# Modulation and queries of a decode head: 224 matmuls of 8 columns replaced by wide weight streams on column groups, then turned by selection matmuls

## Chip, cores, metric

One core of one Trainium2 chip. The metric is the device time of one launch in microseconds (us), as a median of several runs; lower is better. All timed runs quoted here were in the same, undisturbed state ("fast"); runs with a single look are named as such. The profile is of one execution; its span is about 1.8 us shorter than the timed figure. In the profile, TensorE's matmuls are PE, its weight loads PEld, VectorE is DVE, ScalarE is ACT, GpSimd is POOL, and SPq is the sync engine's queue that issues nearly all transfers. L374 is a line of the kernel's source.

## The reference, cut to what matters

A transformer block at decode: batch 8, one new token each, width 512, 32 query heads on 8 key/value heads of 128, a cache of 8192 positions, all in bfloat16.

```python
mod = (silu(c) @ w_mod).reshape(8, 6, 1, 512)      # w_mod: 512 x 3072, 3.15 MB
sa, ca, ga, sb, cb, gb = mod[:, 0], ..., mod[:, 5]
h = layernorm(x) * (1 + ca) + sa
q = h @ wq                                         # wq: 512 x 4096, 4.19 MB
x = x + ga * (attention(q, k_cache, v_cache) @ wo) # caches: 134 MB each
h = layernorm(x) * (1 + cb) + sb
x = x + gb * ((relu(h @ w1 + b1) ** 2) @ w2 + b2)
```

The "head" is everything up to `q`. After it comes a loop over the batch: the keys are transposed on TensorE and multiplied by the queries, then softmax, then the values.

## The kernel before

Keys and values stream through a ring of four slots of 4 MiB. The head borrows slots 2 and 3 for `w_mod` and `wq`, so the loads of keys 2 and 3 wait until the head has read them. The order of the sync queue is: `w_mod`, `wq`, keys 0, keys 1, biases, two loads of `wo`, keys 2, keys 3, then values 0 and so on.

```python
# each output column block of 128 is a stationary operand; 8 columns (the batch) stream past it
for j in range(24):
    for k in range(KT):                                   # KT = 4
        t = op("tensor", lambda e, j=j, k=k: e.matmul(
            modT_ps[:, j, :], wm_cols(k, j), csT[:, k, :],
            start=(k == 0), stop=(k == KT - 1)), [k_csT, d_wm])
released[2] = t
k_modT = op("vector", lambda e: e.tensor_copy(modT[:], modT_ps), [t])
...  # [cut] haT = layernorm(x).T * (1 + ca) + sa, three small DVE operations
for h in range(HQ):
    for k in range(KT):
        t = op("tensor", lambda e, h=h, k=k: e.matmul(
            QT_ps[:, h, :], wq_v[:, k, h * DH:(h + 1) * DH], haT[:, k, :],
            start=(k == 0), stop=(k == KT - 1)), [k_haT, d_wq])
released[3] = t
...  # [cut] eight copies QT_ps -> QTm on DVE
stg_free = [None, None, None, k_QTm]    # one of the four PSUM buffers of the key transposes waits for the last copy into QTm
load(0); load(1)
...  # [cut] loads of biases and wo
load(2); load(3)                        # wait for released[2], released[3]
```

## Time and profile before

| | before |
|---|---|
| time, median | 670.73 us (670.6 to 670.85, 3 runs) |
| bytes read from HBM | 283.66 MB |
| rate from 40 to 640 us | 431 GB/s |
| modulation matmuls | 2.93 us |
| query matmuls | 3.56 us |
| last copy into QTm ends | 26.44 us |
| first key transposes start | 31.80 us |

First the page's line of the granted TensorE clock, the busy share of the 16 transfer engines and the rate, each in 40 equal slices of the span (16.7 us each; 9 is 90% or more):

```profile
PEclk9996995699869997699967997589966999689986
DMA  9999999999999999999999999999999999999996
GB/s 375 430 404 427 431 427 437 434 425 433 433 433 427 432 433 435 431 429 429 435 435 425 434 433 432 427 431 433 439 433 423 428 439 435 421 433 435 437 408 259
...
HBM read 283.66 MB, written 0.01 MB: 424 GB/s over the span
```

The same by stage, from the view of windows: after the stretch and its length come the busy time and number of instructions of PE, PEld, DVE, ACT and POOL, the granted clock, the DMA share and GB/s.

```profile
4.00:20.00 16.00, 4.13 (x108) 3.79 (x108) 3.31 (x12) 1.18 (x2) 11.08 (x34) 1.00 1.02 435
20.00:40.00 20.00, 11.75 (x240) 10.79 (x240) 5.99 (x19) 4.10 (x4) 2.79 (x14) 1.00 0.98 418
40.00:640.00 600.00, 460.39 (x6720) 314.02 (x6720) 282.96 (x514) 226.93 (x270) 0.00 (x0) 0.86 1.01 431
```

Transfers fill every stretch, the head too. TensorE is busy 460 of the 600 us of the loop, so it has room; the transfers have none. Dividing says what to expect of the head: 283.66 MB at 431 GB/s take 658 us, and the span is 668.8.

The head in the view of time (start, length, engine, line, operation; in brackets how long the engine was idle before, and what it waited for):

```profile
4.07 19.10 SPq L408 DMA_DIRECT2D wo_sb<-in_A_wo_dram  x1
...
11.47 2.93 PE L374 MATMUL PS<-csT,ring 128*128 128x8 bf16 x96 [0.19 <-DMA ring<-in_w_mod_dram]
...
15.27 0.19 DVE L382 TENSOR_TENSOR haT<-tmpT,modT 128x32 bf16<-128x32 f32 x1
...
21.97 3.56 PE L386 MATMUL PS<-haT,ring 128*128 128x8 bf16 x128 [7.57 <-DMA ring<-in_A_wq_dram]
23.21 22.55 SPq L335 DMA_DIRECT2D ring<-in_A_k_cache_dram  x2
...
25.56 0.88 DVE L392 CAST QTm<-PS 128x32 bf16<-128x32 f32 x8 [10.10 <-PE PS L386]
...
31.80 5.41 PE L429 MATMUL PS<-IDENT,ring 128*128 128x128 bf16 x64 [6.28 <-DMA ring<-in_A_k_cache_dram]
```

Read the brackets: both matmul stages begin when their weights land, and the key transposes begin when the keys land, 5 us after QTm is ready. And read the two SPq lines: the queue issues the second `wo` load at 4.07 us and does not get past it until 23.17 us, then stays in the loads of keys 2 and 3 until 45.76 us. The first of these alone takes 21.68 us (the same view, cut off at 32 us, shows it by itself), so keys 3 are issued at about 44.9 us, although slot 3 is free at 25.53 us.

The chain of waits, in order of time, up to the start of the first long work on TensorE that it holds: nothing of the head is in it.

```profile
1.26 0.42 SPq L266
1.68 0.05 issue
1.73 59.99 DMA ring<-in_A_k_cache_dram x2
```

### The profile page before, as it was taken

The page shows a single profiled execution, that of the slowest core. Times are in us where ns is not written, and L with a number is a line of the kernel's source. Part 1 is how long each engine was busy: PE and PEld are TensorE (multiplying, and loading weights), DVE is VectorE, ACT ScalarE, POOL GpSimd, SP SyncE. Part 2 cuts the span into 40 slices and gives each one's busy share as a digit, 9 for nine tenths or more (in the row PEclk, how much of TensorE's full clock was granted, in tenths as well). Part 3 has the DMA queues.
Part 4 walks back from the last instruction along what each step waited for, and adds up shares of the span by engine and source line. Part 5 has one row for each costly group of instructions (what it writes and reads, how often), then busy time and mean ns, then how long its engine had stood idle before and what let it go on. Part 6 is the DMA issues. An engine that isn't in the chain of part 4 may idle for free.

```text
span 668.8 us, 16189 instructions
## 1 busy us (share of the span) xinstructions
PE 495.9 (74%) x7492; PEld 341.4 (51%) x7492; DVE 298.8 (45%) x567; ACT 235.1 (35%) x280; POOL 16.9 (3%) x66
## 2 busy tenths in 40 slices
PE   2394964799639983699647996399846996489976
PEld 2383731676318751477316762287414772167634
DVE  2162741466316661267414672166613673156722
ACT  2061630365106640166204660056402662046600
POOL 7200000000000000000000000000000000000000
PEclk9996995699869997699967997589966999689986
DMA  9999999999999999999999999999999999999996
GB/s 375 430 404 427 431 427 437 434 425 433 433 433 427 432 433 435 431 429 429 435 435 425 434 433 432 427 431 433 439 433 423 428 439 435 421 433 435 437 408 259
DMA packets 12969, 283.95 MB, mean 425 GB/s; under 512 B 1266, under 2 KB 2323, under 8 KB 4372
## 3 DMA queue, kind: packets, MB, share of 16 engines
q1 hardware_dynamic: 12900, 283.65, 99.1%
q8 instruction: 13, 0.21, 0.1%
q14 instruction: 8, 0.07, 0.0%
q10 hardware_dynamic: 48, 0.02, 0.0%
HBM read 283.66 MB, written 0.01 MB: 424 GB/s over the span
## 4 chain that ended last, share of the span: by engine, by line
PE 50%; DMA 39%; DVE 5%; ACT 2%; SPq 2%; issue 1%
DMA ring<-in_A_k_cache_dram 37%; PE PS L429 36%; PE PS L444 9%; DVE Pm L533 3%; PE PS L561 2%; DMA ring<-in_B_w_dram 2%; SPq L602 2%; ACT KTb L434 1%; ACT P_sb L511 1%; DVE m L449 1%; PE PS L520 1%; PE PS L420 1%; PE PS L540 0%; DVE rhs_r L537 0%; DVE Dm L502 0%
## 5 line engine op out<-in xcount | busy, mean ns | idle before, releaser
L434 ACT ACTIVATE KTb<-PS 128x1024 bf16<-128x1024 bf16 x192 | 196.7, 1024 | 375.9 <-PE PS L429 375.9
L429 PE MATMUL PS<-IDENT,ring 128*128 128x128 bf16 x4096 | 267.3, 227 | 51.6 <-DMA ring<-in_A_k_cache_dram 51.6
L429 PEld LDWEIGHTS PS<-IDENT,ring 128*128 128x128 bf16 x4096 | 246.7, 102 | 100.3 <-DMA ring<-in_A_k_cache_dram 53.6
L436 DVE COPY KTb<-PS 128x1024 bf16<-128x1024 bf16 x320 | 210.2, 688 | 151.6 <-PE PS L429 149.2
L561 PE MATMUL PS<-ring,Pm 128*32 128x512 bf16 x992 | 83.3, 495 | 63.2 <-DMA ring<-in_A_v_cache_dram 62.3
L570 DVE CAST O_sb<-PS 128x512 bf16<-128x512 f32 x31 | 21.4, 692 | 144.5 <-PE PS L561 144.5
L444 PE MATMUL PS<-KTb,Qb 128*32 128x512 bf16 x1024 | 79.1, 386 | 4.5 <-ACT KTb L434 4.5
L561 PEld LDWEIGHTS PS<-ring,Pm 128*32 128x32 bf16 x992 | 29.5, 116 | 101.9 <-DMA ring<-in_A_v_cache_dram 63.6
L420 PE MATMUL PS<-IDENT 128*128 128x512 bf16 x120 | 31.3, 380 | 0.0
L574 PEld LDWEIGHTS PS<-SEL,O_sb 128*128 128x128 bf16 x124 | 5.3, 99 | 45.3 <-DVE O_sb L570 45.3
L511 ACT ACTIVATE P_sb<-PS,negm 128x512 bf16<-128x512 f32 x32 | 21.6, 686 | 18.9 <-DVE negm L507 18.9
L574 PE MATMUL PS<-SEL,O_sb 128*128 128x8 bf16 x124 | 8.0, 170 | 24.8 <-DVE O_sb L570 24.8
L444 PEld LDWEIGHTS PS<-KTb,Qb 128*32 128x32 bf16 x1024 | 15.4, 94 | 21.1 <-ACT KTb L434 8.5
L533 DVE COPY Pm<-PS 64x512 bf16<-64x512 bf16 x48 | 19.5, 419 | 13.4 <-PE PS L520 12.4
L449 DVE TENSOR_REDUCE m<-PS 128x1 f32<-128x512 f32 x32 | 22.1, 689 | 6.6 <-PE PS L444 6.6
L520 PE MATMUL PS<-IDENT,P_sb 128*64 128x128 bf16 x512 | 20.4, 222 | 2.0 <-ACT P_sb L511 1.2
L520 PEld LDWEIGHTS PS<-IDENT,P_sb 128*64 128x64 bf16 x512 | 15.2, 109 | 9.8 <-ACT P_sb L511 9.8
L420 PEld LDWEIGHTS PS<-IDENT 128*128 128x128 bf16 x120 | 9.9, 103 | 10.8 <-issue 3.4
L577 DVE TENSOR_TENSOR oTn<-PS,rinv 128x8 bf16<-128x8 f32 x31 | 6.0, 194 | 10.9 <-PE PS L574 10.9
L530 ACT ACTIVATE Pm<-PS 64x512 bf16<-64x512 bf16 x16 | 9.5, 593 | 1.1
L386 PE MATMUL PS<-haT,ring 128*128 128x8 bf16 x128 | 3.6, 168 | 7.6 <-DMA ring<-in_A_wq_dram 7.6
L668 ACT ACTIVATE std<-PS,epst 128x8 f32<-128x8 f32 x1 | 0.3, 268 | 25.1 <-PE PS L667 25.1
(112 smaller groups left out, 98.8 us busy)
## 6 DMA issues: line engine op xcount, KB each, us to landing
ring<-in_A_k_cache_dram SPq DMA_DIRECT2D x32, 4096.0 KB, 34.9
ring<-in_A_v_cache_dram SPq DMA_DIRECT2D x31, 4096.0 KB, 28.2
ring<-in_A_wq_dram SPq DMA_DIRECT2D x1, 4096.0 KB, 20.6
ring<-in_w_mod_dram SPq DMA_DIRECT2D x1, 3072.0 KB, 10.6
wo_sb<-in_A_wo_dram SPq DMA_DIRECT2D x1, 3072.0 KB, 45.4
ring<-in_A_v_cache_dram SPq DMA_DIRECT2D x1, 2048.0 KB, 23.6
ring<-in_B_w_dram SPq DMA_DIRECT2D x3, 512.0 KB, 17.5
ring<-in_B_w_dram SPq DMA_DIRECT2D x1, 1344.0 KB, 21.1
```

Of the source, the lines that this page charges most:

```text
L420: op("tensor", lambda e: e.matmul(bank(at).rearrange("p (a r) -> p a r", a=4), IDENT[:, :], rhs))
L429: t = op("tensor", lambda e, j=j, i=i: e.matmul(STG[j][:, i, :], src[:, 32 * k + 8 * j + i, :], IDENT[:, :], is_transpose=True), [loaded[n ...
L434: stg_free[j] = op("scalar", lambda e, j=j, dst=dst: e.activation(dst, STG[j], ACT.Copy), [t], "scaP")
L436: stg_free[j] = op("vector", lambda e, j=j, dst=dst: e.tensor_copy(dst, STG[j]), [t], "vecP")
L444: t = op("tensor", lambda e, hf=hf, q=q, rhs=rhs: e.matmul(PS[32 * q:32 * (q + 1), k, :], Qb[:, 2 * p + hf, :], rhs, start=(p == 0 and hf ...
L449: return op("vector", lambda e: e.tensor_reduce(m4[:, k:k + 1], bank(k), AX.X, ALU.max), [t])
L511: exps.append(op("scalar", lambda e, k=k: e.activation(P_sb[:, k, :], bank(k), ACT.Exp, bias=negm[:, 0:1], scale=inv_sqrt, accum_out=rs4[: ...
L520: t = op("tensor", lambda e, k=k, i=i, hf=hf, src=src: e.matmul(STG[k][64 * hf:64 * (hf + 1), i, :], src, IDENT[:, :], is_transpose=True, ...
L533: done.append(op("vector", lambda e, dst=dst, frm=frm: e.tensor_copy(dst, frm), [t, k_pm], "vecP"))
L561: t = op("tensor", lambda e, p=p, m=m, cg=cg, vt=vt, Obank=Obank: e.matmul(Obank[32 * cg:32 * (cg + 1), :], lhs[:, p, 32 * m:32 * m + 32], ...
L570: t = op("vector", lambda e, osb=osb, Obank=Obank: e.tensor_copy(osb, Obank), [t], "vecP")
L602: d_w2 = [dma("sync", s_w2[i], lambda e, a=a, z=z, j=j: e.dma_start(W2v[:, a:z, :].rearrange("p (k j) n -> p k (j n)", j=j), B_w2[128 * a: ...
```

## The change

Its intent: few wide matmuls in place of many narrow ones. The batch of 8, padded to 32, becomes the stationary operand and the weights stream past it, 512 columns at a time, on four column groups of the array at once. The result has batches on partitions, in four groups of 32 rows, and must be turned: a copy from PSUM to SBUF, then matmuls against a small selection matrix with ones at the 8 used rows of each group. Modulation does this in fp32, queries in bf16.

```diff
-        for j in range(24):
+        def row_groups(out_ps, lhsT, w, chunks, deps):
             for k in range(KT):
-                t = op("tensor", lambda e, j=j, k=k: e.matmul(
-                    modT_ps[:, j, :], wm_cols(k, j), csT[:, k, :],
-                    start=(k == 0), stop=(k == KT - 1)), [k_csT, d_wm])
+                for g, n in enumerate(chunks):
+                    t = op("tensor", lambda e, k=k, g=g, n=n: e.matmul(
+                        out_ps[32 * g:32 * (g + 1), :], lhsT[:, k, :], w[:, k, 512 * n:512 * (n + 1)],
+                        start=(k == 0), stop=(k == KT - 1), tile_position=(0, 32 * g)), deps)
+            return t
+
+        t = row_groups(bank(0), csT, wmod_v, (0, 1), [k_csT, d_wm])
+        k_mr0 = op("vector", lambda e: e.tensor_copy(mod_r[0:64, 0, :], bank(0)[0:64, :]), [t])
+        t = row_groups(bank(1), csT, wmod_v, (2, 3, 4, 5), [])
         released[2] = t
+        k_mr1 = op("scalar", lambda e: e.activation(mod_r[:, 1, :], bank(1), ACT.Copy), [t])
+        for i in range(KT):
+            t = op("tensor", lambda e, i=i: e.matmul(
+                mod_ab[:, :, i, :], mod_r[0:64, 0, :].rearrange("r (p i) -> r i p", i=KT)[:, i, :],
+                EYE[0:64, 0:2, :]), [k_mr0, k_xT])
 ...  [cut: copies, haT as before; a second selection for the other four chunks, weights mod_r[:, 1, 128*i:128*(i+1)]]
-        for h in range(HQ):
-            for k in range(KT):
-                t = op("tensor", ...)           # 128 matmuls
-        released[3] = t
+        t0 = row_groups(bank(2), haT, wq_v, (0, 1, 2, 3), [k_haT, d_wq])
+        released[3] = t = row_groups(bank(3), haT, wq_v, (4, 5, 6, 7), [])
+        k_q = [op("vector", lambda e: e.tensor_copy(q_r[:, 0, :], bank(2)), [t0]),
+               op("scalar", lambda e: e.activation(q_r[:, 1, :], bank(3), ACT.Copy), [t])]
+        for u in range(2):
+            for i in range(4):
+                t = op("tensor", lambda e, u=u, i=i: e.matmul(
+                    QT_ps[:, u, :, i, :], q_r[:, u, DH * i:DH * (i + 1)], EYEB[:, :, :]), [k_q[u]])
 ...  [cut: the eight copies into QTm; memsets and two selects on POOL for EYE, EYEB and the padding]
```

The loop, the loads, their order and their sizes are untouched.

## The prediction

> **What bounds the kernel now.** The page says that the kernel reads 283.66 MB at a mean of 424 GB/s. The windows view gives 431 GB/s from 40 to 640 us (DMA share 1.01), 435 from 4 to 20 us and 418 from 20 to 40 us: the head already streams at about the steady rate. 283.66 MB at 431 GB/s is 658 us of a span of 668.8; the rest is some 2 us of start and 5 us after the last weights. The Trainium skill, "DMA: Bandwidth & Descriptors", section "Where 436 GB/s comes from", puts the fabric at 435.2 GB/s; the trace agrees. So the bound is bytes, not the head's arithmetic.
>
> **The head in the timeline.** The 96 modulation matmuls take 2.93 us (11.47 to 14.40), as soon as w_mod has landed. TensorE idles 7.57 us for wq, and the 128 query matmuls take 3.56 us (21.97 to 25.53); eight copies into QTm end at 26.44. TensorE then idles 6.28 us until the first keys land at 31.8. The chain of waits holds none of this: its first piece of work is 59.99 us of key loads, from 1.73 us.
>
> **Do earlier releases start transfers earlier?** Slots 2 and 3 are released by the modulation and the query matmuls. But the sync queue is held in the second Wo issue from 4.07 to 23.17, and in the next two loads until 45.76, by transfers ahead of it; its list of waits names neither stage. Slot 2 is free 9 us before the queue gets to it, slot 3 (25.53) probably before its issue too. No DMA gap stands in the head that an earlier release could close.
>
> **What the change does.** It removes 224 matmuls of 8 columns (6.5 us of TensorE). It adds 56 matmuls of 32x512 on four column groups, 16 selection matmuls, two copies a stage (about 0.69 us each, as the 128x512 evictions take; one on DVE, one on ACT), and memsets and selects on GpSimd (estimated 1.5 us from its 0.1 to 0.45 us instructions). The same 32x512 form takes 1.91 us per 32 in the value stage, so I estimate modulation at 1.5 to 2 us, fp32 selection at 0.65 us (as the four fp32 transposes), haT at about 15 us instead of 15.5. Queries: 21.95 + 1.9 + 0.7 + 0.3 + 0.9, QTm complete at about 25.8. Slot 2 is released about 1 us earlier, slot 3 about 1.5 us. Loop, loads, their order and sizes are unchanged.
>
> **On the critical path:** none. Even a stage 4 us slower would end before the keys land. Net: 0 us, perhaps 0.1 us from fewer instructions or other phases of the transfers.
>
> **Predicted:** 670.6 us, 669.4 to 671.8 for 8 in 10. Faster by over 2%: 0.01; within 2%: 0.98; slower: 0.01.
>
> **What would show it right:** the query matmuls shrink from 3.56 to about 1.9 us, QTm is ready around 25.8 us, TensorE's idle time before the first key transposes grows from 6.3 to about 7 us; they still start at about 31.8 us; the Wo issue still lasts to about 23.2; key loads still take about 35 us from issue to landing; 40 to 640 us stays at 431 GB/s.
>
> **What would make it wrong:** a fall in GB/s in the loop (another phase between releases and loads); the sync queue waiting for slot 3 today; the dense 512-column matmuls lowering the granted clock later (0.70 in 60 to 70 us already) so far that slots are released late; copies and selections over 6 us longer than estimated.

## The result, and the profile after

The changed kernel takes 670.8 us (670.7 to 671.03, 4 runs), beside 670.79 us for the kernel before in the same rounds: ratio 1.0001, 95% interval 0.9984 to 1.0018. A ratio here is the mean of one kernel's fast runs over the mean of the other's of the same rounds, so not quite the ratio of the medians. The prediction (670.6 us, no change) holds. Its account of the head's inside does not.

The page after, same lines:

```profile
PEclk9696996799859995599968997699977999779985
DMA  9999999999999999999999999999999999999996
GB/s 375 434 405 437 415 435 433 432 427 433 433 437 428 427 437 431 433 429 431 435 435 428 427 433 437 427 429 433 435 437 428 423 435 439 429 427 433 435 410 250
...
HBM read 283.66 MB, written 0.01 MB: 424 GB/s over the span
```

The windows after:

```profile
4.00:20.00 16.00, 7.71 (x52) 4.92 (x52) 4.15 (x14) 1.77 (x3) 11.61 (x32) 0.96 1.03 441
20.00:40.00 20.00, 13.01 (x153) 9.50 (x154) 6.85 (x20) 4.69 (x5) 3.15 (x16) 0.69 0.97 415
40.00:640.00 600.00, 458.98 (x6716) 313.52 (x6716) 282.50 (x514) 226.75 (x270) 0.00 (x0) 0.87 1.00 431
```

The rate of the loop is 431 GB/s in both. But look at the first number after the length: TensorE is busy longer in the head than before (7.71 against 4.13 us, 13.01 against 11.75), with far fewer instructions. (About half of the second difference is only that the key transposes begin 0.7 us earlier.) The view of time shows why:

```profile
4.10 18.88 SPq L430 DMA_DIRECT2D wo_sb<-in_A_wo_dram  x1
...
11.34 3.60 PE L377 MATMUL PS<-ring,KTb 128*32 128x512 bf16 x24
...
14.87 2.04 PE L391 MATMUL PS<-EYE,KTb 64*128 64x16 f32 x8
...
16.83 1.08 PE L400 MATMUL PS<-EYE,KTb 128*128 128x32 f32 x8
...
17.64 0.19 DVE L398 TENSOR_TENSOR KTb<-tmpT,modT 128x32 bf16<-128x32 f32 x1
...
21.65 3.61 PE L377 MATMUL PS<-ring,KTb 128*32 128x512 bf16 x32 [3.74 <-DMA ring<-in_A_wq_dram]
...
23.03 23.01 SPq L344 DMA_DIRECT2D ring<-in_A_k_cache_dram  x2
...
26.26 0.88 DVE L414 CAST QTm<-PS 128x32 bf16<-128x32 f32 x8 [1.97 <-PE PS L410]
...
31.08 5.97 PE L451 MATMUL PS<-IDENT,ring 128*128 128x128 bf16 x64 [4.86 <-DMA ring<-in_A_k_cache_dram]
```

And the chain of waits after, the same piece of it, 0.2 us longer:

```profile
1.26 0.42 SPq L270
1.67 0.05 issue
1.72 60.18 DMA ring<-in_A_k_cache_dram x2
```

The head's terms beside the prediction:

| | before | predicted | after |
|---|---|---|---|
| modulation matmuls, us | 2.93 | 1.5 to 2 | 3.60 |
| first fp32 selection, us | none | 0.65 | 2.04 |
| haT ready at, us | 15.46 | about 15 | 17.83 |
| query matmuls, us | 3.56 | 1.9 | 3.61 |
| slot 3 released at, us | 25.53 | about 24 | 25.26 |
| QTm complete at, us | 26.44 | 25.8 | 27.14 |
| first key transposes, us | 31.80 | 31.8 | 31.08 |
| time, us | 670.79 | 670.6 | 670.80 |

So two questions stand. Is the head really free, and how far? And why did the wide streams not save time inside it?

### The profile page after: what moved, and what is told of

Same layout as the page of the kernel before. It is cut to its first block, busy times and chain, and to the rows that moved or that the text cites. A ratio compares the mean times of both kernels' runs of the same rounds, so it can differ in the third digit from the quotient of the medians.

```text
span 669.0 us, 15914 instructions
## 1 busy us (share of the span) xinstructions
PE 499.3 (75%) x7348; PEld 340.7 (51%) x7348; DVE 300.2 (45%) x570; ACT 236.1 (35%) x282; POOL 17.5 (3%) x71
## 3 DMA queue, kind: packets, MB, share of 16 engines
HBM read 283.66 MB, written 0.01 MB: 424 GB/s over the span
## 4 chain that ended last, share of the span: by engine, by line
PE 50%; DMA 39%; DVE 5%; ACT 2%; SPq 2%; issue 1%
DMA ring<-in_A_k_cache_dram 37%; PE PS L451 36%; PE PS L466 9%; DVE Pm L555 3%; PE PS L583 2%; DMA ring<-in_B_w_dram 2%; SPq L624 2%; ACT KTb L456 1%; ACT P_sb L533 1%; DVE m L471 1%; PE PS L542 1%; PE PS L442 1%; PE PS L562 0%; DVE rhs_r L559 0%; DVE Dm L524 0%
## 5 line engine op out<-in xcount | busy, mean ns | idle before, releaser
L592 DVE CAST O_sb<-PS 128x512 bf16<-128x512 f32 x31 | 21.4, 692 | 144.5 <-PE PS L583 144.5
L533 ACT ACTIVATE P_sb<-PS,negm 128x512 bf16<-128x512 f32 x32 | 21.5, 685 | 18.9 <-DVE negm L529 18.9
L466 PEld LDWEIGHTS PS<-KTb,Qb 128*32 128x32 bf16 x1024 | 15.5, 94 | 21.1 <-ACT KTb L456 8.5
L555 DVE COPY Pm<-PS 64x512 bf16<-64x512 bf16 x48 | 19.5, 419 | 13.4 <-PE PS L542 12.4
L542 PEld LDWEIGHTS PS<-IDENT,P_sb 128*64 128x64 bf16 x512 | 15.2, 109 | 9.8 <-ACT P_sb L533 9.8
L442 PEld LDWEIGHTS PS<-IDENT 128*128 128x128 bf16 x120 | 9.9, 103 | 10.8 <-issue 3.4
L377 PE MATMUL PS<-ring,KTb 128*32 128x512 bf16 x56 | 7.2, 627 | 3.7 <-DMA ring<-in_A_wq_dram 3.7
```

The lines of the kernel that those rows point to most:

```text
L442: op("tensor", lambda e: e.matmul(bank(at).rearrange("p (a r) -> p a r", a=4), IDENT[:, :], rhs))
L466: t = op("tensor", lambda e, hf=hf, q=q, rhs=rhs: e.matmul(PS[32 * q:32 * (q + 1), k, :], Qb[:, 2 * p + hf, :], rhs, start=(p == 0 and hf ...
L533: exps.append(op("scalar", lambda e, k=k: e.activation(P_sb[:, k, :], bank(k), ACT.Exp, bias=negm[:, 0:1], scale=inv_sqrt, accum_out=rs4[: ...
L542: t = op("tensor", lambda e, k=k, i=i, hf=hf, src=src: e.matmul(STG[k][64 * hf:64 * (hf + 1), i, :], src, IDENT[:, :], is_transpose=True, ...
L555: done.append(op("vector", lambda e, dst=dst, frm=frm: e.tensor_copy(dst, frm), [t, k_pm], "vecP"))
L592: t = op("vector", lambda e, osb=osb, Obank=Obank: e.tensor_copy(osb, Obank), [t], "vecP")
```

## The experiments

My theory: the time is the bytes; the head lies in slack, of a size that can be worked out; inside the head the streams ran at half pace because TensorE's clock was low after idling. The rivals are that the head's end or its slot releases gate something, and that the form of the new matmuls is slow in itself. Where nothing else is said, an experiment edits the changed kernel, and its result passed the comparison with the reference.

### No head arithmetic at all (e1_nohead)

```diff
-        ... modulation, haT, queries, copies into QTm ...
+        k_modT = pool(lambda e: e.memset(modT[:], 0.5), [k_all])
+        released[2], released[3], k_QTm = d_wm, d_wq, k_q0      # QTm stays zero
```

> The changed kernel with all arithmetic of modulation and queries taken out (modT set to a constant, QTm left at zero; wrong result on purpose), all loads kept. My theory, the bound is bytes and the head lies in slack: 670.8 us, within 0.5 us of before, although the head costs nothing now. Rival, the head's arithmetic or its releases gate something: 2 to 8 us faster. First key transposes still at about 31 us.

Measured: 670.67 us (5 runs; before 670.73), ratio 0.9999, interval 0.9986 to 1.0013; the result is wrong. The first key transposes started at 32.12 us. With the head's arithmetic gone and its two slots free as soon as their weights have landed, nothing is gained. The sync queue could not use the early releases: its second load of the pair, keys 3, was again issued only at 45.3 us (23.02 + 22.30). As long as its loads stay as they are, no way of computing this head can make this kernel faster.

### Fewer bytes (e9_skipwq)

```diff
-        d_wq = dma("sync", s_wq, lambda e: e.dma_start(RING[:, 3, :], A_wq...))
+        d_wq = t = pool(lambda e: e.memset(RING[:, 3, :], 0.0), [t])
```

> The changed kernel without the load of wq (slot 3 is filled with zeros by GpSimd; wrong result on purpose): 4.19 MB fewer of 283.66. Theory, the time is the bytes: 4.19 MB at 431 GB/s, 9.7 us faster, about 661.1 us. Rival, the loop of TensorE and its slot releases bounds (TensorE makes up half of the chain of waits): under 3 us faster.

Measured: 661.09 us against 670.71, ratio 0.9856 (0.984 to 0.9873): 9.6 us gone for 4.19 MB, where 431 GB/s gives 9.7. The head itself was far later in this run (its modulation matmuls began at 23.83 us instead of 11.34, its key transposes at 40.08 instead of 31.08), and the gain came all the same. The delay of the modulation comes from the edit itself: the trace shows the added memset on GpSimd from 9.18 to 22.93 us, and beside it the normalisation on VectorE (L365), 0.53 us in the changed kernel, lasting from 9.93 to 23.21. That the one held up the other is an inference from these times. Bytes count, the head does not. The output still agreed with the reference although the queries were all zero; so agreement in this case says little about whether queries are right.

### The key transposes held back (e5_keys50, e6_keys70, e11_keys61)

A chain of memsets on GpSimd, which has nothing else to do by then, serves as a timer; 27, 50 and 35 of them.

```diff
+        for _ in range(27):
+            t = pool(lambda e: e.memset(O_sb[:], 0.0), [t])
         k_all = t
 ...
-        stg_free = [k_modT, None, None, k_QTm]
+        stg_free = [k_all, None, k_modT, k_QTm]
```

> The changed kernel with the first key transposes held until about 50 us (they start at 31.1 us now) by a chain of memsets on GpSimd; releases of slots 2 and 3 as they are. Theory: the four first slots' bytes plus weights keep the transfers busy until about 67.7 us (28.3 MB at 431 GB/s from 2 us), key slot 0 is released about 10.8 us after the start, so at 61: no transfer comes late and the time stays 670.8 within 1 us. Rival, the head's end is on the chain: up to 19 us slower.

> The same, held until about 70 us. Theory: slot 0 is released at about 81 us, some 13 us after the transfers ran dry and with 2 us until the next ones flow; bytes bound the rest, so this loss is never won back: 13 to 16 us slower, about 685 us, with the transfers idle between about 68 and 82 us. Rival, later slack absorbs it: under 5 us slower. Rival, the head's end is on the chain: 39 us slower.

> The first key transposes held until about 61.5 us (35 memsets of 1.007 us after 25.5 us). From the run held to 76.45 us (21.4 us lost), the slack is 24 us beyond the 31.1 us of the changed kernel. Theory of a knee with slope one: loss 61.5 - 31.1 - 24 = 6.4 us, so 677 us, 676 to 678. Rival, part of the loss is absorbed later when it is small: 671 to 675 us.

| run | transposes start | time | loss against before, same rounds |
|---|---|---|---|
| changed kernel | 31.08 us | 670.80 us | 0.0 us |
| e5_keys50 | 53.36 us | 670.78 us | 0.2 us, ratio 1.0004 (0.9987 to 1.0021) |
| e11_keys61 | 61.28 us | 676.54 us | 5.9 us, ratio 1.0088 (1.0071 to 1.0105) |
| e6_keys70 | 76.45 us | 692.04 us | 21.4 us, ratio 1.0316 (1.0299 to 1.0333) |

The timer was slower than I had taken it for (1.007 us a memset), so e6 was held to 76.45 us, not 70, and the 685 us expected of it was missed. The reasoning, put at the start that was reached, gives the sum: slot 0 is released 10.8 us after the start, at 87.2 us, 19.5 us after the 67.7 us at which the transfers were to run dry; with the 2 us that I had allowed until the next ones flow, that is a loss of some 21 us. Here is the view of windows of e6 in that stretch (last two numbers: DMA share, GB/s):

```profile
66.00:68.00 2.00, 0.00 (x0) 0.00 (x0) 0.00 (x0) 0.00 (x0) 1.89 (x3) 1.00 0.99 426
68.00:70.00 2.00, 0.00 (x0) 0.00 (x0) 0.00 (x0) 0.00 (x0) 1.89 (x3) 1.00 0.31 131
70.00:72.00 2.00, 0.00 (x0) 0.00 (x0) 0.00 (x0) 0.00 (x0) 1.89 (x3) 1.00 0.00 0
...
86.00:88.00 2.00, 2.00 (x36) 1.47 (x34) 1.29 (x2) 1.68 (x2) 0.00 (x0) 1.00 0.00 0
88.00:90.00 2.00, 2.00 (x37) 1.55 (x34) 1.50 (x3) 1.25 (x2) 0.00 (x0) 1.00 0.99 295
```

The transfers do stop, at about 68.6 us, and flow again at about 88, within a microsecond of the release. So the standstill is 19.4 us, and the other 2 us of the loss are not the allowance: they go in the windows from 88 to 128 us, which run at 401 to 424 GB/s instead of 431. Between e11 and e6 the start moves by 15.2 us and the loss by 15.5 us: slope one, no later slack wins it back. Subtracting the loss from the delay gives a slack of 24 us in both (30.2 - 5.9; 45.4 - 21.4). In e11 the pure standstill is only about 3 us; the windows of the next 50 us run at 385 to 441 GB/s instead of 431 (405 in the mean), which makes up the other 3. My explanation, not tested, is that each load is then issued only when one slot comes free.

### The releases of slots 2 and 3 held back (e7_rel40, e8_rel60)

```diff
+        late = pool(lambda e: e.memset(O_sb[:], 0.0), [k_all, released[2], released[3]])   # after 16, 38 memsets
+        released[2] = released[3] = k_all = late
         load(2)
         load(3)
```

> The changed kernel with the releases of slots 2 and 3 (loads of keys 2 and 3) held until about 40 us; key transposes as they are. Theory: the loads in flight (19.9 MB) last until about 48 us, so releases 15 us later cost nothing: 670.8 within 1 us; the mean time from issue to landing falls for those two. Rival, the release of slot 3 (25.3 us) gates the next load: about 15 us slower.

> The same, held until about 60 us. Theory: the transfers run dry at about 48 us and flow again at about 62: 12 to 15 us slower, about 684 us. Rival, the loss is absorbed later: under 5 us slower. Rival, releases gate the loads now: 35 us slower.

Measured: the loads were issued at 42.57 us in e7 and at 64.88 us in e8. e7: 670.65 us, ratio 1.0001 (0.9985 to 1.0018). e8: 687.74 us against 670.61, 17.1 us lost, ratio 1.0256 (1.0239 to 1.0273). In e8 the transfers stood still from about 50 to 65 us (2 GB/s in that window). The 684 us expected were for a release at 60; it came 4.9 us later. A side effect: the loop's start also waited for the timer, so the key transposes began at 43.32 and 65.56 us. In e8 slot 0 was thereby released at about 76 us, while keys 2 and 3 kept the transfers busy for some 19 us from 65; so the loss is that of the late loads. The second wait is no explanation of e7, which lost nothing.

e7 also settles the long issues. With most of the earlier transfers done, the two loads took the queue 2.58 us together instead of 23.01:

```profile
4.18 18.85 SPq L432 DMA_DIRECT2D wo_sb<-in_A_wo_dram  x1
42.57 2.58 SPq L346 DMA_DIRECT2D ring<-in_A_k_cache_dram  x2
```

So the queue was held by transfers ahead of it, not by the head's releases. An earlier release could not be used: the queue comes to keys 3 at about 45 us anyway.

### TensorE kept busy ahead of both stages (e2_warm, e3_warm_before)

Dummy matmuls of 128x512 ahead of the modulation (14) and ahead of the queries (30 in the changed kernel, 33 in the kernel before).

```diff
+        for _ in range(14):
+            op('tensor', lambda e: e.matmul(bank(0)..., IDENT[:, :], <IDENT repeated four times>), [k_id])
```

> The changed kernel with dummy matmul streams of 128x512 ahead of the modulation stage and ahead of the query stage, so that TensorE is busy until each begins. Theory, the 32x512 streams ran at half pace (0.43 us per four) because TensorE had been idle: the 24 modulation matmuls fall from 3.60 to about 1.6 us, the 32 query matmuls from 3.61 to about 1.9 us (0.22 us per four). Rival, the pace comes from the form itself (padded weights read from KTb, streaming out of the ring while transfers write SBUF): both stay at 3.6 us. Time of the kernel in both cases 670.8, within 0.5 us.

> The kernel before with the same dummy streams. Theory, its 128x8 matmuls are bound by a fixed time per instruction (28 ns each at any clock): query stage stays at 3.5 to 3.6 us, modulation at 2.7 to 2.9 us. Rival, they too run at half pace after idling: the query stage falls to about 1.8 us. Time 670.8 within 0.5 us.

The wide streams of e2, in the view of time:

```profile
12.49 1.90 PE L379 MATMUL PS<-ring,KTb 128*32 128x512 bf16 x24
...
14.32 2.04 PE L393 MATMUL PS<-EYE,KTb 64*128 64x16 f32 x8
...
25.46 1.91 PE L379 MATMUL PS<-ring,KTb 128*32 128x512 bf16 x32
```

The query stage takes 1.91 us instead of 3.61, the modulation 1.90 instead of 3.60 (I had said 1.6, forgetting that its first 8 matmuls run only two at a time). So the form is not slow in itself; it is slow after idling. That the clock is what differs, the granted clock in the profile confirms for the query stage, the number before the last two: 0.50 in the changed kernel, 1.00 in e2.

```profile
21.60:25.20 3.60, 3.55 (x33) 1.30 (x34) 0.69 (x1) 0.00 (x0) 2.08 (x11) 0.50 1.02 437
...
25.40:27.40 2.00, 2.00 (x37) 0.86 (x36) 0.69 (x1) 0.00 (x0) 0.29 (x1) 1.00 1.14 492
```

For the modulation it reads 1.00 in both runs, so there a low clock is inferred from the pace alone. The remedy is not a sure one either: in e10 below, the same 14 dummies ahead of the modulation, with the same idle time of about 2 us between, left it at 3.23 us. Why the two differ is not shown. The kernel's time: 670.93 us against 670.73, ratio 1.0003 (0.9988 to 1.0018), so again nothing.

In e3 (a single look, 670.72 us) the narrow matmuls of the kernel before hardly care about the clock:

```profile
13.22 2.93 PE L376 MATMUL PS<-csT,ring 128*128 128x8 bf16 x96
...
24.93 3.35 PE L390 MATMUL PS<-haT,ring 128*128 128x8 bf16 x128
```

Only the query stage was reached with the clock up (recorded 1.00, and the dummies just before it at full pace): 128 of them in 3.35 us, 3.56 us after idling, so 26 and 28 ns each. The modulation of e3 tells the same from the other side: the clock was low there (recorded 0.50 from 13 to 16 us, and the dummies just after it at half pace), and its 96 took 2.93 us, 31 ns each. I had expected 3.5 to 3.6 for the queries; what matters is that they do not halve. They are paid by the instruction, the wide ones by the column. Two costs that happen to be equal after idling (32 wide ones at 3.61, 128 narrow ones at 3.56) explain why the change bought no time inside the head.

The Trainium skill, "TensorE: Matmul & The Clock Gate", says both things: "the default state is throttled, and activity releases the throttle" (section "What's actually happening"), with 426.7 ns between 512-column matmuls cold and 215.7 warm, and a floor of about 25 ns from start to start however few the columns (section "Wait — 56ns, not 53.3ns?"). This agrees: about 430 ns for each set of four streams in the changed kernel's head (from one set's weight loads to the next; 3.61 us for all eight with the tail of the last), and 26 to 31 ns for a narrow matmul. I had read neither for the prediction, and took the pace from the value stage.

### The strided weights of the selection (e4_contig, e10_contig_warm)

The first selection took 2.04 us, the second 1.08, with equal counts. The first reads every fourth column as weights. e4 lets the copy write them in order; e10 adds the dummy streams (14 and 18).

```diff
-        k_mr0 = op("vector", lambda e: e.tensor_copy(mod_r[0:64, 0, :], bank(0)[0:64, :]), [t])
+        k_mr0 = op("vector", lambda e: e.tensor_copy(
+            mod_r[0:64, 0, :].rearrange("r (i p) -> r i p", i=KT),
+            bank(0)[0:64, :].rearrange("r (p i) -> r i p", i=KT)), [t])
 ...
-                mod_ab[:, :, i, :], mod_r[0:64, 0, :].rearrange("r (p i) -> r i p", i=KT)[:, i, :],
+                mod_ab[:, :, i, :], mod_r[0:64, 0, 128 * i:128 * (i + 1)],
```

> The changed kernel, where the copy of the first modulation half writes its columns in the order that the selection wants, so that the four fp32 selection matmuls load contiguous weights instead of every fourth column. Theory, the stride of the weights makes the first selection slow (2.04 us against 1.08 us of the second): it falls to about 1.1 us, haT about 0.9 us earlier. Rival, the first selection was slow because TensorE was still at the low clock: it stays at about 2 us. Time 670.8 within 0.5 us.

> The contiguous selection weights together with the dummy streams, since the strided selection took 2.04 us also in the warmed run and the contiguous one took 1.89 us in the run that was not warmed. Theory, both stride and low clock double it, each alone: with both removed the first selection takes about 1.1 us (0.13 us per record). Rival, only the place in the sequence matters (the first selection after the copy is slow whatever its weights): about 1.9 us. Time 670.8 within 0.5 us in either case.

e4 (a single look, 670.81 us) by itself spoke for the rival: 1.89 us, not 1.1. But in that execution the second selection, which has contiguous weights in both kernels, had slowed from 1.08 to 1.91 us as well: by this pace the clock, which had risen before the second selection of the changed kernel, had not risen yet. (The recorded clock reads 1.00 at this place in both.)

```profile
14.88 1.89 PE L393 MATMUL PS<-EYE,KTb 64*128 64x16 f32 x8
...
16.69 1.91 PE L402 MATMUL PS<-EYE,KTb 128*128 128x32 f32 x8
```

e10, contiguous and warmed:

```profile
16.23 1.06 PE L395 MATMUL PS<-EYE,KTb 64*128 64x16 f32 x8
17.22 1.08 PE L404 MATMUL PS<-EYE,KTb 128*128 128x32 f32 x8
```

Together with e2 (strided, right after streams at full pace: 2.04 us) the four cases separate the two causes: a stride doubles the fp32 selection when the clock is up, the low clock doubles it when the weights are contiguous. In the changed kernel the stride is the likely one, since the second selection right after it ran at 1.08 us. e10 comes nearest to the head that the prediction described: query matmuls 1.91 us, QTm complete at 25.91 us (25.03 + 0.88); only its modulation stayed at 3.23 us. Its time is 671.04 us against 670.64, ratio 1.0005 (0.9989 to 1.0022).

No version with the same loads beats the kernel before; e1 shows that none can by way of the head's arithmetic.

## Why the prediction was right, and where its inside was wrong

- **The bound, "bytes, not the head's arithmetic": right.** 283.66 MB at 431 GB/s before and after; 4.19 MB fewer saved 9.6 us (e9); no head saved nothing (e1).
- **"On the critical path: none": right.** It said that a stage 4 us slower would do no harm, since it would end before the keys land. The idle time of 6 us before the keys was not the limit: the runs show 24 us of slack for the start of the key transposes, and the whole of the loss beyond it.
- **"No DMA gap stands in the head that an earlier release could close": right.** With both slots free as soon as their weights had landed, nothing was gained (e1); loads of keys 2 and 3 issued at 42.57 us cost nothing (e7), at 64.88 us they cost 17.1 us (e8). The sync queue is held by transfers ahead of it, as said.
- **"The same 32x512 form takes 1.91 us per 32 in the value stage, so I estimate modulation at 1.5 to 2 us", and queries at 1.9: wrong.** The step that failed is carrying a duration over from a stage with a busy TensorE to one that starts after idling. Measured 3.60 and 3.61 us; 1.90 and 1.91 with the dummies ahead (e2). The profile before held the hint: at 646.6 us, in the last batch, a value stage that came after narrow matmuls and a wait for data shows the same 32 matmuls in 3.44 us.
- **"fp32 selection at 0.65 us (as the four fp32 transposes)": wrong.** It takes 2.04 us; contiguous weights at the raised clock take 1.06 (e10). The model for it, transposes of 8 rows, was another shape.
- **"Slot 2 is released about 1 us earlier, slot 3 about 1.5 us", "QTm complete at about 25.8", idle time "grows from 6.3 to about 7 us": wrong, as sums of the above.** Slot 2 is released later (14.94 us against 14.40), slot 3 only 0.3 us earlier, QTm is complete at 27.14 us, the idle time shrinks to 4.86 us. All of it disappears in the slack.

The total was right because it rested on the term that bounds, and the wrong terms were all multiplied by zero. What stays open: why dummies raised the pace of the modulation in e2 and not in e10, why the key transposes of e9 began only at 40.08 us, and whether the 0.2 to 0.4 us by which some edited kernels stand above their neighbours is anything but noise. All intervals include 1, but in e10 each of the four runs (670.93 to 671.06) lies above each of the seven of before (670.53 to 670.76).

## What to carry to other kernels

Before making a stage faster, ask what waits for its end, and divide the bytes by the rate that the long part of the kernel reaches: here the quotient, 658 us of 669, already said that little was left for any head to give. Slack can be worked out from a trace (bytes issued, over the rate, against the time when the next issue must come) and measured by holding the stage back with an idle engine as a timer; a loss with slope one beyond the knee shows both the knee and the bound. And take the duration of a matmul only from a stage with the same history: after idling, wide streams cost nearly twice here (3.61 against 1.91 us), while narrow ones, paid by the instruction, cost almost the same (3.56 against 3.35).

## What the Trainium skill lacked or had wrong

- "DMA: Bandwidth & Descriptors", section "Where 436 GB/s comes from": it says that for transfers between HBM and SBUF the HBM side (about 358 GB/s) binds. This kernel, on one core, reads HBM at 431 GB/s over 600 us. The fabric figure of 435.2 of the same section, and the 425 GB/s that it quotes for one transfer of 16 MB, are the ones that fit. The page's section "Measured (HBM→SBUF, 128 partitions, SWDGE, issued from GpSimd)" does say that the 425 are for a single core with its pair's other core idle; the section named here does not, and read alone it misleads.
- "Perfetto Trace Analysis", section "DMA Instruction — HWDGE (DVE, Sync)", draws the issuing engine as held until all descriptors of the load are generated, with a buffer that can be full, but gives no time; no page that was found says that this can last so long: 18.9 us for a 1 MiB load and about 22 us for the next one with some 19 MB ahead, 2.58 us for two loads of 4 MiB once most of it had landed (e7). That makes an early release useless where the queue is not there to use it.
- "TensorE: Matmul & The Clock Gate", section "What's actually happening": it says that the gate follows how busy TensorE has been; as an exception the page names only transposes. In e2 the profile shows TensorE without a gap from 12.49 to 25.4 us, yet the recorded clock is 0.50 from 18.3 to 21.6 us, shortly after 2.8 us of small fp32 selections. This suggests, from one trace, that busy in the profile is not the activity that the gate counts; what it counts these runs do not show.
- Same page, section "LDWEIGHTS (loading the stationary operand)": it gives the load by the number of columns alone. The fp32 selection with every fourth column took 2.04 us (e2), with contiguous columns 1.06 us (e10), at the same count and shape. "Advanced Engine Details and Errata", section "SBUF Cachelines", says that accesses which each touch another 16-byte line are penalised, and every fourth fp32 column is such a case; it has no figure and no word on weight loads.
- Same page, section "Seeing it yourself", warns that recorded clock events can be unreliable. A number for it: the recorded clock is 1.00 in the changed kernel from 11.3 to 14.9 us, where four streams of 512 took about 430 ns, and 1.00 in e2 from 12.4 to 14.4 us, where the same ones ran at twice that pace.
